# Sliding-window attention and a gated FFN on one core: separate PSUM tensors for single banks, key copies on ScalarE

## The chip, the core and the metric

The kernel runs on one core of a Trainium2 chip. Engines of a core run their own instruction queues in order and meet at semaphores: TensorE (PE: matmuls; PEld: its weight loads), VectorE (DVE), ScalarE (ACT), GpSimd (POOL) and SyncE (SP), which here issues the transfers from and to device memory. PE writes its results to PSUM, eight banks of 2 KB per partition; DVE and ACT read them from there. The metric is the device time of one execution in microseconds; the measured time before is the median of three runs.

## The reference

```
scores = scale * q @ k^T ; keep = (pos_k < 4) | (0 <= pos_q - pos_k < 128)
a = softmax(where(keep, scores, -1e9)) ; x = a @ v        # 4 batches, 8 heads, 768 positions, head size 64
y = (relu(X @ w_gate) * (X @ w_val)) @ w_out              # X: 3072 x 512, d_ff 1536
```

Each position attends to the first four keys ("sink") and to the 128 keys up to itself. The heads are then put side by side and go through the FFN.

## The kernel before

Two heads make a pair; there are 16 pairs (`U[0]` to `U[15]`), four to a batch. For a pair, `T` transposes keys and queries on PE (8 + 8 transposes, keys first) into PSUM and copies them to SBUF: the keys into `kE` by five copies (L178 and L181 on DVE, L180 twice on ACT, and L183 on DVE, which copies the four sink columns from `kE` itself to three further places), the queries into `qT` by one copy on DVE (L182). `Sg(u, g)`, three for a pair, makes the scores of a window group (L196) in both banks of a two-bank tensor, and ACT takes their exponentials (L200); DVE multiplies them by a mask (L202), except in the head, where a bias matmul (L192) masks them. `V(u, part)`, two for a pair, multiplies by the values into one bank and by ones into the other, for the row sums (L213); DVE then transposes the sums, inverts them, transposes back and multiplies (L219 to L223) into `xT`.

`chunk(b, g, m)` is the first FFN layer for 384 positions and 128 of the 1536 columns: four gate matmuls (L235) into bank `gp`, the relu on ACT into `gs` (L238), four value matmuls (L240) into bank `vp`, and the product of `gs` and `vp` on DVE into `hT` (L242). The banks `gp` and `vp` go round three: bank 0 and 1 of `ps0` and bank 0 of `ps1` (`GV`). `ffn2` is one of twelve matmuls of the second layer (L255) into bank 1 of `ps1` (`OP`); after the twelfth, ACT copies the result (L259) and SP stores it.

All eight banks are four tensors `ps0` to `ps3` of two banks. In the head, `T`, `Sg` and `V` go round all four (`nextps`); afterwards round `ps2` and `ps3`.

The order is written out by hand. The head does pairs 0 to 3, then loads and casts the FFN weights. Then come 96 slots, one per chunk: batch 0 in slots 0 to 23, batch 1 from slot 24 on, and so on. After its chunk a slot runs steps of the attention of the next batch in the order T, S, S, S, V, V for each pair: from slot 12 to 23 two steps a slot (pairs 4 to 7), from slot 24 to 71 one step a slot (pairs 8 to 15), after that none. From slot 24 on a slot ends with three `ffn2` matmuls. The 72 that are left over run at the end without a chunk. The waits on the semaphores are put in by the framework, from the tensors that an instruction reads and writes.

Of the kernel before, what the change touches and what calls it, by code (L numbers as in the profile page):

```python
# [9 lines left out]
F32 = mybir.dt.float32  # L10
# [9 lines left out]
def kernel(  # L20
# [48 lines left out]
    mb = const.tile([128, 3, 512], BF16, name="mb")  # L69
    PS = [pspool.tile([128, 2, 512], F32, name=f"ps{i}") for i in range(4)]  # L70
    GV = [PS[0][:, 0, :], PS[0][:, 1, :], PS[1][:, 0, :]]

# [86 lines left out]

    rot = [0]  # L160
    banks = [PS]

    def nextps():
        rot[0] += 1
        return banks[0][rot[0] % len(banks[0])]

    def T(u):
        t = u.i % NT
        ps = nextps()[:].bitcast(BF16)
        for j, x in ((1, kn[u.i % 2]), (0, qn[u.i % 2])):  # L170
            for n in range(NR):
                nc.tensor.transpose(ps[:, j, 96 * n:96 * n + 96],  # L172
                                    x[0:PR, n, :, :].rearrange("p h d -> p (h d)"), ident[0:PR, 0:PR])
        vk, vq = (ps[:, j, 0:768].rearrange("d (b p) -> d p b", p=PR) for j in (1, 0))
        n_ = dict(b=8)
        to = lambda ap: ap.rearrange("d (p b) -> d p b", **n_)
        e = kE[t]
        nc.vector.tensor_copy(to(e[:, 0:128]), vk[:, 0:16])  # L178
        for i in range(2):
            nc.scalar.copy(to(e[:, 132 + 252 * i:380 + 252 * i]), vk[:, 16 + 31 * i:47 + 31 * i])  # L180
        nc.vector.tensor_copy(to(e[:, 636:780]), vk[:, 78:96])  # L181
        nc.vector.tensor_copy(to(qT[t][:]), vq)  # L182
        nc.vector.tensor_copy(e[:, 128:884].rearrange("d (i c) -> d i c", c=252)[:, :, 0:4],  # L183
                              e[:, 0:4].unsqueeze(1).to_broadcast([128, 3, 4]))

    def Sg(u, g, bias=False):
        t = u.i % NT
        n, segs = SEG[g]
        ps = nextps()
        if bias:  # L190
# [71 lines left out]
    with tc.manual_schedule():  # L262
# [132 lines left out]
```

## Time and profile before

| | before |
|---|---|
| median of 3 runs (lowest to highest) | 359.69 us (357.64 to 360.26) |
| profiled execution: time, span | 357.96 us, 356.3 us |
| PE busy | 276.0 us (77%) |
| DVE busy | 173.6 us (49%) |
| ACT busy | 116.0 us (33%) |
| POOL busy | 71.9 us (20%) |
| mean granted PE clock | 0.951 |
| chain that ended last: PE, DVE, ACT | 59%, 16%, 8% |

The span is the time between the first and the last instruction of the profile. A group of matmuls is drawn to its modelled end, so that the next group can start before the drawn end of the one ahead of it. "Idle <- X" at a row names what ended the idle time in front of it.

### The profile page before, as it was taken

Reading aid. Unit: us, or ns where it says so; the run is one execution under the profiler, and the core shown is the slowest. Engines: PE = TensorE matmul, PEld = TensorE weight load, DVE = VectorE, ACT = ScalarE, POOL = GpSimd, SP = SyncE. Lnnn points to the kernel's source line nnn. Section 1 sums busy time; section 2 is a strip of 40 time slices with the busy share of each in tenths; the row PEclk is TensorE's granted clock in tenths of the full one; section 3 lists DMA queues with packets and bytes.
Section 4 is the critical chain, followed back from the end, with each engine's and each line's share of the span. In section 5 each row is a group of like instructions: output and inputs, shape, how many; then the busy total and the mean of one; then the engine's idle time right before and its main releaser. Section 6 shows DMA issues by size and latency. Waiting matters only on the chain.

```text
span 356.3 us, 5404 instructions
## 1 busy us (share of the span) xinstructions
PE 276.0 (77%) x2114; PEld 148.3 (42%) x2136; DVE 173.6 (49%) x348; ACT 116.0 (33%) x202; POOL 71.9 (20%) x90
## 2 busy tenths in 40 slices
PE   1868287655965888898888889897989788878895
PEld 1336143324533444454444535353545344434442
DVE  4677623268557665656464737465646122221100
ACT  2535022232442443434334352425152222222211
POOL 5366500893033030303030302100000000000000
PEclk9989679969888799999999999999999999999999
DMA  8999999399560005107230520000000000000032
GB/s 200 237 272 351 286 210 309 137 234 193 113 136 0 2 1 154 33 10 163 92 74 31 138 56 3 31 29 0 31 31 29 0 31 29 29 29 31 2 118 88
DMA packets 44105, 35.14 MB, mean 99 GB/s; under 512 B 27184, under 2 KB 33328, under 8 KB 44080
## 3 DMA queue, kind: packets, MB, share of 16 engines
q1 hardware_dynamic: 44080, 34.81, 38.6%
q8 instruction: 16, 0.26, 0.3%
q14 instruction: 9, 0.07, 0.1%
HBM read 28.51 MB, written 6.29 MB: 98 GB/s over the span
## 4 chain that ended last, share of the span: by engine, by line
PE 59%; DVE 16%; ACT 8%; issue 5%; DMA 5%; SPq 2%; POOL 2%; ACTq 0%; DVEq 0%; POOLq 0%
PE ps L255 17%; PE ps L240 15%; PE ps L235 14%; PE ps L213 5%; PE ps L196 4%; DVE hT L242 4%; ACT gs L238 4%; DVE qT L182 3%; PE ps L172 3%; DMA wst<-in_moe_w_out_dram 3%; DMA vf<-in_v_dram 2%; ACT kE L180 2%; ACT ot L259 2%; DVE R L221 2%; DVE t L219 2%
## 5 line engine op out<-in xcount | busy, mean ns | idle before, releaser
L242 DVE TENSOR_TENSOR hT<-gs,ps 128x384 bf16<-128x384 f32 x96 | 53.1, 553 | 104.9 <-PE ps L240 104.4
L240 PE MATMUL ps<-xT,wv 128*128 128x384 bf16 x384 | 81.9, 337 | 21.5 <-ACT gs L238 20.7
L235 PE MATMUL ps<-xT,wg 128*128 128x384 bf16 x384 | 82.6, 339 | 14.4 <-DVE xT L223 6.8
L238 ACT ACTIVATE gs<-ps 128x384 f32<-128x384 f32 x96 | 47.1, 491 | 127.3 <-PE ps L235 126.4
L255 PE MATMUL ps<-wo,hT 128*128 128x512 bf16 x266 | 71.4, 380 | 10.1 <-DVE hT L242 8.9
L240 PEld LDWEIGHTS <-wv 128*128 128x128 bf16 x384 | 38.5, 100 | 56.8 <-issue 35.9
L200 ACT ACTIVATE ee<-ps 128x1006 bf16<-128x1006 f32 (+2 forms) x48 | 45.1, 961 | 40.7 <-PE ps L196 40.7
L235 PEld LDWEIGHTS <-wg 128*128 128x128 bf16 x384 | 37.4, 100 | 50.3 <-issue 21.8
L111 POOL CAST kn<-kf 96x1024 bf16<-96x1024 f32 x16 | 16.6, 1035 | 115.8 <-PE ps L172 112.7
L255 PEld LDWEIGHTS <-hT 128*128 128x128 bf16 x288 | 25.0, 97 | 35.3 <-issue 13.9
L202 DVE TENSOR_TENSOR ee<-ee,msk 128x1006 bf16<-128x1006 bf16 (+2 forms) x36 | 25.2, 700 | 28.6 <-ACT ee L200 28.4
L196 PE MATMUL ps<-qT,kE 64*128 64x251 bf16 (+4 forms) x224 | 21.7, 281 | 16.5 <-DVE qT L182 13.8
L196 PEld LDWEIGHTS <-kE 64*128 64x128 bf16 x224 | 10.5, 101 | 35.4 <-issue 30.0
L180 ACT COPY kE<-ps 128x248 bf16<-128x248 bf16 x32 | 10.1, 369 | 41.2 <-DVE kE L178 41.1
L259 ACT COPY ot<-ps 128x512 f32<-128x512 f32 x24 | 14.0, 583 | 27.3 <-PE ps L255 24.2
L219 DVE STREAM_TRANSPOSE t<-ps 128x384 f32<-128x384 f32 x32 | 18.6, 580 | 5.9 <-PE ps L213 4.8
L221 DVE STREAM_TRANSPOSE R<-r 128x384 f32<-128x384 f32 x32 | 18.5, 578 | 1.1
L223 DVE TENSOR_TENSOR xT<-ps,R 128x384 bf16<-128x384 f32 x32 | 17.8, 557 | 1.1
L213 PE MATMUL ps<-ee,vn 128*64 128x255 bf16 (+8 forms) x288 | 16.1, 236 | 0.9 <-DVE xT L223 0.9
L104 POOL CAST vn<-vf 128x896 bf16<-128x896 f32 x16 | 14.8, 926 | 8.2 <-DMA vf<-in_v_dram 8.2
L213 PEld LDWEIGHTS <-vn 128*64 128x64 bf16 x288 | 12.5, 110 | 7.6 <-issue 7.2
L213 PE MATMUL ps<-ee,ones 128*64 128x255 bf16 (+8 forms) x288 | 15.6, 233 | 0.0
(43 smaller groups left out, 144.1 us busy)
## 6 DMA issues: line engine op xcount, KB each, us to landing
kf<-in_k_dram SPq DMA_DIRECT2D x16, 384.0 KB
qf<-in_q_dram SPq DMA_DIRECT2D x16, 384.0 KB
vf<-in_v_dram SPq DMA_DIRECT2D x32, 192.0 KB
out_dram<-ot SPq DMA_DIRECT2D x24, 256.0 KB
wst<-in_moe_w_gate_dram SPq DMA_DIRECT2D x6, 512.0 KB
wst<-in_moe_w_val_dram SPq DMA_DIRECT2D x6, 512.0 KB
wst<-in_moe_w_out_dram SPq DMA_DIRECT2D x3, 1024.0 KB
vf<-in_v_dram SPq DMA_DIRECT2D x16, 12.0 KB
```

What stands on the lines that cost most here:

```text
L196: nc.tensor.matmul(out=ps[:, h, c0:c1], lhsT=kE[t][64 * h:64 * h + 64, x0:x0 + 128], rhs=qT[t][64 * h:64 * h + 64, q0:q0 + c1 - c0], start ...
L200: nc.scalar.activation(x, ps[:, :, 0:n], Act.Exp, bias=0.0, scale=scale)
L202: nc.vector.tensor_tensor(x, x, msk[:, g, 0:n].unsqueeze(1).to_broadcast([128, 2, n]), op=Alu.mult)
L213: nc.tensor.matmul(out=ps[64 * h:64 * h + 64, which, o0:o0 + c1 - c0], lhsT=w, rhs=ee[u.i % NE][:, g, h, c0:c1], start=i == 0, stop=i == l ...
L219: nc.vector.transpose(out=t1[:], in_=ps[:, 1, 0:CUT])
L221: nc.vector.transpose(out=R[:].rearrange("p (c e) -> p c e", e=32), in_=r[:].unsqueeze(2).to_broadcast([128, CUT // 32, 32]))
L235: nc.tensor.matmul(out=gp[:, 0:CUT], lhsT=wg[:, ko, m * 128:(m + 1) * 128], rhs=x[:, ko, c], start=ko == 0, stop=ko == KO - 1)
L238: nc.scalar.activation(gs[:], gp[:, 0:CUT], Act.Relu, bias=0.0, scale=1.0)
L240: nc.tensor.matmul(out=vp[:, 0:CUT], lhsT=wv[:, ko, m * 128:(m + 1) * 128], rhs=x[:, ko, c], start=ko == 0, stop=ko == KO - 1)
L242: nc.vector.tensor_tensor(h[:, m, c], gs[:], vp[:, 0:CUT], op=Alu.mult)
L255: nc.tensor.matmul(out=op, lhsT=hT[b % 2][:, m, t * 128:(t + 1) * 128], rhs=wo[:, m, :], start=m == 0, stop=m == FM - 1)
L259: nc.scalar.copy(ot[:], op)
```

## The change

The eight banks are cut differently: two tensors of two banks, `PP` (`pp0`, `pp1`), and four of one bank, `G` (`g0` to `g3`). The first layer of the FFN goes round `g0`, `g1`, `g2`, the second layer writes `g3`: the same number of banks for each as before, each now with a tensor of its own. The scores take a whole `PP` tensor. `T` transposes the keys into one tensor and the queries into another, and `V` puts values and sums, in the head, into two `G` tensors; after the head, `V` takes both banks of one `PP` tensor, and `T` one bank of each. In the head, `T` and `V` go round the `G` tensors and the scores round the two `PP` tensors. All key copies of a pair, that of the sink columns too, go to ACT; the query copy stays on DVE and comes first.

```diff
-    PS = [pspool.tile([128, 2, 512], F32, name=f"ps{i}") for i in range(4)]
-    GV = [PS[0][:, 0, :], PS[0][:, 1, :], PS[1][:, 0, :]]
+    PP = [pspool.tile([128, 2, 512], F32, name=f"pp{i}") for i in range(2)]
+    G = [pspool.tile([128, 512], F32, name=f"g{i}") for i in range(4)]
...
-    def nextps():
-        rot[0] += 1
-        return banks[0][rot[0] % len(banks[0])]
+    def pair():
+        rot[0] += 1
+        return PP[rot[0] % 2]
+
+    def two():
+        if head[0]:
+            srot[0] += 2
+            return G[srot[0] % 4][:], G[(srot[0] + 1) % 4][:]
+        x = pair()
+        return x[:, 0, :], x[:, 1, :]
...
     def T(u):
-        ps = nextps()[:].bitcast(BF16)
-        for j, x in ((1, kn[u.i % 2]), (0, qn[u.i % 2])):
+        tk, tq = two() if head[0] else (pair()[:, 0, :], pair()[:, 0, :])
+        for x, ps in ((kn[u.i % 2], tk), (qn[u.i % 2], tq)):
...
-        nc.vector.tensor_copy(to(e[:, 0:128]), vk[:, 0:16])
+        nc.vector.tensor_copy(to(qT[t][:]), vq)
+        nc.scalar.copy(to(e[:, 0:128]), vk[:, 0:16])
         for i in range(2):
             nc.scalar.copy(to(e[:, 132 + 252 * i:380 + 252 * i]), vk[:, 16 + 31 * i:47 + 31 * i])
-        nc.vector.tensor_copy(to(e[:, 636:780]), vk[:, 78:96])
-        nc.vector.tensor_copy(to(qT[t][:]), vq)
-        nc.vector.tensor_copy(e[:, 128:884].rearrange("d (i c) -> d i c", c=252)[:, :, 0:4],
-                              e[:, 0:4].unsqueeze(1).to_broadcast([128, 3, 4]))
+        nc.scalar.copy(to(e[:, 636:780]), vk[:, 78:96])
+        nc.scalar.copy(e[:, 128:884].rearrange("d (i c) -> d i c", c=252)[:, :, 0:4],
+                       e[:, 0:4].unsqueeze(1).to_broadcast([128, 3, 4]))
...
-        gp, vp = GV[gvn[0] % 3], GV[(gvn[0] + 1) % 3]
+        gp, vp = G[gvn[0] % 3], G[(gvn[0] + 1) % 3]
...
-    OP = [[PS[1][:, 1, :]], [PS[1][:, 1, :], PS[2][:, 0, :], PS[3][:, 0, :]]]
+    OP = [[G[3][:]], [G[3][:], PP[0][:, 0, :], PP[1][:, 0, :]]]
```

`Sg` takes `pair()` where it took `nextps()`, and `V` takes `two()`. Because lines are added, L172 becomes L180, L196 L203, L200 L207, L213 L220, L235 L242, L238 L245, L240 L247, L242 L249, L255 L262 and L259 L266.

No engine's instructions change in number or place but for those of `T` on DVE and ACT. What changes elsewhere are the waits. The first place is PE in the last FFN batch (slots 80 and 81), the first matmul of each group and what it waits for. Before (`wg`: gate, `wv`: value, `wo`: second layer; the number of a semaphore's name means nothing):

```order
L235 MATMUL ps0_110<-xT1_102,wg_98 128x384 [waits DVE_49]
...
L240 MATMUL ps1_111<-xT1_102,wv_99 128x384 [waits Activation_49]
...
L255 MATMUL ps1_111<-wo_100,hT0_103 128x512 [waits DVE_49]
...
L235 MATMUL ps0_110<-xT1_102,wg_98 128x384 [waits Activation_49]
...
L240 MATMUL ps0_110<-xT1_102,wv_99 128x384 [waits Activation_49]
```

After:

```order
L242 MATMUL g1_113<-xT1_102,wg_98 128x384 [waits DVE_49]
...
L247 MATMUL g2_114<-xT1_102,wv_99 128x384 [waits Activation_49]
...
L262 MATMUL g3_115<-wo_100,hT0_103 128x512 [waits Activation_49]
...
L242 MATMUL g0_112<-xT1_102,wg_98 128x384 [waits DVE_49]
...
L247 MATMUL g1_113<-xT1_102,wv_99 128x384 [waits Activation_49]
```

The same rows in the same order, but the second-layer matmul no longer waits for DVE, and the value matmuls of the last row write a tensor (`g1`) that the gate matmuls ahead of them (`g0`) do not write and their relu does not read.

The second place is `T` of pair 5 on DVE, between the product of one chunk and the next one's. Before:

```order
L242 TENSOR_TENSOR hT0_103<-gs_881,ps0_110 128x384 [waits PE_49,Activation_49]
L178 COPY kE2_87<-ps3_113 128x128 [waits PE_49]
L181 COPY kE2_87<-ps3_113 128x144 [waits Activation_49]
L182 COPY qT2_84<-ps3_113 128x768
L183 COPY kE2_87<-kE2_87 128x3x4 [waits DVE_49]
L202 TENSOR_TENSOR ee2_90<-ee2_90,msk_108 128x2x503 [waits Activation_49]
```

After:

```order
L249 TENSOR_TENSOR hT0_103<-gs_883,g1_113 128x384 [waits PE_49,Activation_49]
L185 COPY qT2_84<-pp1_111 128x768 [waits PE_49]
L209 TENSOR_TENSOR ee2_90<-ee2_90,msk_108 128x2x503 [waits Activation_49]
L249 TENSOR_TENSOR hT0_103<-gs_931,g0_112 128x384 [waits PE_49,Activation_49]
L209 TENSOR_TENSOR ee2_90<-ee2_90,msk_108 128x2x499 [waits Activation_49]
```

Three copies left DVE's queue, and the query copy follows the product of the chunk at once. On ACT, at the same place, before:

```order
L238 ACTIVATE gs_881<-ps0_110 128x384 [waits PE_49,Activation_49]
L180 COPY kE2_87<-ps3_113 128x248 [waits DVE_49]
L180 COPY kE2_87<-ps3_113 128x248
L200 ACTIVATE ee2_90<-ps2_112 128x2x503 [waits PE_49]
L238 ACTIVATE gs_929<-ps1_111 128x384 [waits PE_49,Activation_49]
```

After (the row that ends in x2 stands for the two copies of 248 columns):

```order
L245 ACTIVATE gs_883<-g0_112 128x384 [waits PE_49]
L186 COPY kE2_87<-pp0_110 128x128 [waits DVE_49,PE_49]
L188 COPY kE2_87<-pp0_110 128x248 x2
L189 COPY kE2_87<-pp0_110 128x144
L190 COPY kE2_87<-kE2_87 128x3x4 [waits Activation_49]
L207 ACTIVATE ee2_90<-pp0_110 128x2x503 [waits PE_49]
```

The copies now stand on ACT in one run, and wait for PE and an earlier instruction of DVE, not for a copy of the same pair on DVE.

The third place is PE at `T` of pair 5 and the scores behind it. Before (first key transpose, first query transpose, then the loads and the matmul of the scores):

```order
L172 MATMUL ps3_113<-ident_105,kn1_94 128x96 [waits DVE_49]
...
L172 LDWEIGHTS qn1_92 [waits Pool_49]
...
L196 LDWEIGHTS kE2_87 [waits DVE_49]
L196 MATMUL ps2_112<-qT2_84,kE2_87 128x255 [waits DVE_49]
...
L196 LDWEIGHTS kE2_87 [waits DVE_49,Activation_49]
```

After:

```order
L180 MATMUL pp0_110<-ident_105,kn1_94 128x96 [waits DVE_49]
...
L180 MATMUL pp1_111<-ident_105,qn1_92 128x96 [waits DVE_49]
...
L203 LDWEIGHTS kE2_87 [waits DVE_49,Activation_49]
L203 MATMUL pp0_110<-qT2_84,kE2_87 128x255 [waits Activation_49]
...
L203 LDWEIGHTS kE2_87 [waits Activation_49]
```

The query transposes go to the other tensor and got a wait on DVE of their own; the scores now wait for ACT's copies too where they waited for DVE's.

## Rows read from the trace of the kernel before

**Rows 1.** By stretch: us; PE, PEld, DVE, ACT, POOL busy; clock; DMA; GB/s
```profile
41.70:70.50 28.80, 21.85 (x104) 10.69 (x103) 7.20 (x13) 6.38 (x13) 8.48 (x10) 0.88 0.95 224
70.50:125.50 55.00, 37.61 (x361) 22.19 (x361) 37.26 (x71) 18.98 (x32) 19.55 (x24) 0.81 0.53 110
125.50:276.00 150.50, 128.88 (x1045) 71.18 (x1060) 88.01 (x170) 57.47 (x100) 20.34 (x24) 1.00 0.20 54
276.00:336.30 60.30, 48.49 (x247) 24.13 (x249) 12.79 (x24) 14.21 (x28) 0.00 (x0) 1.00 0.06 22
```
**Rows 2.** What PE waited for from 125.5 to 337 us: total, times, longest
```profile
PE ps L240 <- ACT gs L238: 14.7, 23, 0.6
PE ps L255 <- DVE hT L242: 8.9, 16, 0.7
PE ps L235 <- ACT ot L259: 4.1, 6, 0.7
PE ps L196 <- DVE qT L182: 2.4, 8, 0.3
PE ps L196 <- DVE kE L183: 1.5, 6, 0.3
```
**Rows 3.** PE's timeline, last FFN batch: start, length, instructions, [idle <-releaser]
```profile
285.89 0.81 PE L255 MATMUL ps<-wo,hT 128*128 128x512 bf16 x3
...
287.26 0.81 PE L240 MATMUL ps<-xT,wv 128*128 128x384 bf16 x4
288.79 0.81 PE L255 MATMUL ps<-wo,hT 128*128 128x512 bf16 x3 [0.72 <-DVE hT L242]
289.44 0.81 PE L235 MATMUL ps<-xT,wg 128*128 128x384 bf16 x4
290.89 0.81 PE L240 MATMUL ps<-xT,wv 128*128 128x384 bf16 x4 [0.64 <-ACT gs L238]
...
293.63 0.81 PE L255 MATMUL ps<-wo,hT 128*128 128x512 bf16 x3
```
**Rows 4.** Timeline, a middle pair: last V step, transposes, next chunk, first scores
```profile
181.03 0.56 DVE L223 TENSOR_TENSOR xT<-ps,R 128x384 bf16<-128x384 f32 x1
...
182.52 0.50 PE L172 MATMUL ps<-ident,qn 96*128 96x96 bf16 x8
...
184.16 0.81 PE L240 MATMUL ps<-xT,wv 128*128 128x384 bf16 x4
...
185.28 0.28 PE L196 MATMUL ps<-qT,kE 64*128 64x255 bf16 x2 [0.31 <-DVE qT L182]
```
**Rows 5.** Timeline of pair 6, first FFN batch: from V to scores
```profile
98.96 0.56 DVE L223 TENSOR_TENSOR xT<-ps,R 128x384 bf16<-128x384 f32 x1
99.44 0.54 DVE L242 TENSOR_TENSOR hT<-gs,ps 128x384 bf16<-128x384 f32 x1
...
99.90 0.28 DVE L178 COPY kE<-ps 128x128 bf16<-128x128 bf16 x1
100.22 0.63 ACT L180 COPY kE<-ps 128x248 bf16<-128x248 bf16 x2 [2.94 <-DVE kE L178]
...
101.11 0.95 DVE L182 COPY qT<-ps 128x768 bf16<-128x768 bf16 x1
...
102.11 0.45 PE L196 MATMUL ps<-qT,kE 64*128 64x255 bf16 x4 [3.29 <-DVE qT L182]
```
**Rows 6.** Timeline around pair 4: POOL casts, transposes, sink copy
```profile
62.22 2.02 POOL L129 CAST wo<-wst 128x1024 bf16<-128x1024 f32 x2 [17.40 <-DMA wst<-in_moe_w_out_dram]
...
69.47 1.04 POOL L111 CAST kn<-kf 96x1024 bf16<-96x1024 f32 x1
...
70.56 0.51 PE L172 MATMUL ps<-ident,kn 96*128 96x96 bf16 x8 [0.80 <-POOL kn L111]
...
74.17 1.63 DVE L183 COPY kE<-kE 128x12 bf16<-128x12 bf16 x1
```
**Rows 7.** Timeline, the second-layer matmuls at the end
```profile
336.30 16.35 PE L255 MATMUL ps<-wo,hT 128*128 128x512 bf16 x74 [0.72 <-DVE hT L242]
```

More of the change, by code (lines that the diff above doesn't have):

```diff
@@ L158, in setup @@
             nc.vector.tensor_scalar(mb[:, g, 0:n], msk[:, g, 0:n], -1.0, BIG, op0=Alu.add, op1=Alu.mult)
-    rot = [0]
-    banks = [PS]
-    def nextps():
+    rot, srot = [0], [0]
+    head = [True]
+    def pair():
         rot[0] += 1
-        return banks[0][rot[0] % len(banks[0])]
+        return PP[rot[0] % 2]
[5 more added lines that the diff above has]
+        return x[:, 0, :], x[:, 1, :]
     def T(u):
         t = u.i % NT
-        ps = nextps()[:].bitcast(BF16)
-        for j, x in ((1, kn[u.i % 2]), (0, qn[u.i % 2])):
+        tk, tq = two() if head[0] else (pair()[:, 0, :], pair()[:, 0, :])
+        for x, ps in ((kn[u.i % 2], tk), (qn[u.i % 2], tq)):
             for n in range(NR):
-                nc.tensor.transpose(ps[:, j, 96 * n:96 * n + 96],
+                nc.tensor.transpose(ps.bitcast(BF16)[:, 96 * n:96 * n + 96],
                                     x[0:PR, n, :, :].rearrange("p h d -> p (h d)"), ident[0:PR, 0:PR])
-        vk, vq = (ps[:, j, 0:768].rearrange("d (b p) -> d p b", p=PR) for j in (1, 0))
-        n_ = dict(b=8)
-        to = lambda ap: ap.rearrange("d (p b) -> d p b", **n_)
+        vk, vq = (ps.bitcast(BF16)[:, 0:768].rearrange("d (b p) -> d p b", p=PR) for ps in (tk, tq))
         e = kE[t]
-        nc.vector.tensor_copy(to(e[:, 0:128]), vk[:, 0:16])
+        to = lambda ap: ap.rearrange("d (p b) -> d p b", b=NR)
+        nc.vector.tensor_copy(to(qT[t][:]), vq)
+        nc.scalar.copy(to(e[:, 0:128]), vk[:, 0:16])
         for i in range(2):
             nc.scalar.copy(to(e[:, 132 + 252 * i:380 + 252 * i]), vk[:, 16 + 31 * i:47 + 31 * i])
-        nc.vector.tensor_copy(to(e[:, 636:780]), vk[:, 78:96])
-        nc.vector.tensor_copy(to(qT[t][:]), vq)
-        nc.vector.tensor_copy(e[:, 128:884].rearrange("d (i c) -> d i c", c=252)[:, :, 0:4],
-                              e[:, 0:4].unsqueeze(1).to_broadcast([128, 3, 4]))
+        nc.scalar.copy(to(e[:, 636:780]), vk[:, 78:96])
+        nc.scalar.copy(e[:, 128:884].rearrange("d (i c) -> d i c", c=252)[:, :, 0:4],
+                       e[:, 0:4].unsqueeze(1).to_broadcast([128, 3, 4]))
     def Sg(u, g, bias=False):
@@ L188, in Sg @@
         n, segs = SEG[g]
-        ps = nextps()
+        ps = pair()
         if bias:
@@ L206, in V @@
     def V(u, part):
-        ps = nextps()
+        pv, pd = two()
         segs = VSEG[part]
@@ L212, in V @@
                     w = vn[u.i % NV][:, j, h, :] if which == 0 else ones[:]
-                    nc.tensor.matmul(out=ps[64 * h:64 * h + 64, which, o0:o0 + c1 - c0], lhsT=w,
+                    nc.tensor.matmul(out=(pv, pd)[which][64 * h:64 * h + 64, o0:o0 + c1 - c0], lhsT=w,
                                      rhs=ee[u.i % NE][:, g, h, c0:c1], start=i == 0, stop=i == len(segs) - 1,
@@ L218, in V @@
         r = npool.tile([128, CUT // 32], F32, name="r")
-        nc.vector.transpose(out=t1[:], in_=ps[:, 1, 0:CUT])
+        nc.vector.transpose(out=t1[:], in_=pd[:, 0:CUT])
         nc.vector.reciprocal(r[:], t1[:].rearrange("p (c e) -> p c e", e=32)[:, :, 0])
@@ L222, in V @@
                             in_=r[:].unsqueeze(2).to_broadcast([128, CUT // 32, 32]))
-        nc.vector.tensor_tensor(xT[u.b % 2][:, u.p, CUT * part:CUT * part + CUT], ps[:, 0, 0:CUT], R[:], op=Alu.mult)
+        nc.vector.tensor_tensor(xT[u.b % 2][:, u.p, CUT * part:CUT * part + CUT], pv[:, 0:CUT], R[:], op=Alu.mult)
         ready[u.b, u.p, part] = True
@@ L305 @@
             cast_wo(c, c, nc.gpsimd)
-        banks[0] = PS[2:4]
+        head[0] = False
         stages = []
```

## Prediction

> **What bounds the kernel now.** I read the busy time by stretch first, then PE's waits, then the timelines behind the largest waits.
>
> By stretch [rows 1]: from 125.5 us on, PE is 80 to 86% busy at full clock, and DVE (58% and 21%), ACT (38% and 24%) and the transfers (20% and less) are far from full. So PE is the bound there, with holes. From 70.5 to 125.5 PE is 68% busy at a mean clock of 0.81, and DVE 68%: two in-order queues that wait for each other. From 41.7 to 70.5 the transfers are at 95%.
>
> The holes after 125.5 us have names [rows 2]. The largest is the value matmuls (L240) waiting for the relu (L238), 14.7 us in 23 waits. The value matmuls do not use the relu's result; the gate and value banks of that chunk are the two banks of `ps0`. Nor do the second-layer matmuls use the product that they wait for (L255 <- L242, 8.9 us in 16): the one writes a bank of `ps1`, the other reads the other bank. The same holds for the gate matmuls waiting for the output copy (4.1 in 6). These are waits for a neighbour bank of the same tensor.
>
> What a slot costs without them is in [rows 3]: the gate matmuls at 289.44 start 0.65 us after the three second-layer matmuls at 288.79, though these are drawn 0.81 long. So a hole is 0.16 us longer than its row says. The four value matmuls behind gates with no wait take 0.65 too. Three slots take 293.63 - 285.89 = 7.74 us; dense they would take 3 x 3 x 0.65 = 5.9.
>
> **The change part by part.**
>
> *One tensor per bank in the FFN.* The listing of the last batch shows what is left: gate matmuls wait for the DVE product of two chunks earlier (their bank's last reader), value matmuls for the relu of the chunk before, the first second-layer matmul of a block for the output copy. With slots of about 2 us, each of these was done a slot ago or, for the output copy, within the next chunk's 1.3 us (the gates right behind it wait 4.1 / 6 = 0.7 us for it now). I cost them at nothing. Removed: the five lines of [rows 2] are 31.6 us in 59 waits, and 59 x 0.16 = 9.4 us behind them, 41 in all. The other way round, PE is idle for 150.50 + 60.30 - 128.88 - 48.49 = 33.4 us of the two stretches [rows 1], and with the same 9.4 that makes 42.8. Of these the last batch has 8 x (7.74 - 5.9) = 14.7 (24 slots), which leaves 28 for the 8 pairs of the middle: a pair there goes from 150.5 / 8 = 18.8 to 15.3 us. I take 43.
>
> *The copies of T, after 125.5 us.* The last two lines of [rows 2] (2.4 and 1.5, counted above) are the scores waiting for query and sink copy. ACT's run of five copies is not in the trace as a whole. The two of 248 columns take 0.63 [rows 5]. Each of the three new ones (128 and 144 columns, and 12) costs at least 0 and at most half of that, 0.32: the run is 0.63 to 1.6. I take 1.3, nearest to the upper end, since a small copy has a fixed part. Its cover is what PE does between the last key transpose and the scores: from 182.52 to 184.16 + 0.65 = 184.81, 2.29 us [rows 4]. Hidden; the relu of the next chunk waits behind the run, but its reader on PE comes a chunk later. DVE loses three copies per pair that were on nobody's path here.
>
> *A new wait.* The query transposes now go to the tensor that the last V step leaves, and wait for its last DVE instruction. Behind them on PE stand the second layer and the next chunk. In [rows 4] that instruction ends at 181.03 + 0.56 = 181.59; the transposes start at 182.52, of which 0.64 us is a relu wait (a line like the last L240 of [rows 3]) that goes: 181.88. Slack 0.29. Cost 0, at most 0.3 x 8 = 2.4.
>
> *Pairs 4 to 7, 70.5 to 125.5 us.* Here the scores follow `T` at once, so the copies are on the path. Before [rows 5]: the product ends at 99.98, then key copy, ACT's two copies, key copy, query copy one after the other, and the scores start at 102.11. After: the query transposes may start when V's last step ends, 99.52, take 0.34 (drawn 0.50 in [rows 4], less the 0.16) and about 0.2 until DVE has them, the copy takes 0.95: 101.0. That is 1.1 us for each of pairs 5, 6 and 7, 3.3 in all; ACT's run, at most 1.6 from 0.34 earlier on, ends at about the same time. For pair 4 the sink copy, which took 1.63 us on DVE beside POOL's casts [rows 6], also goes to ACT: 1.63, less some 0.4 that the first scores cover, and the 1.1 as for the others, about 2.3. The last chunk of the stretch loses a relu wait: 0.8. Together 6.4. Bounds: 3, if only pair 4 and a part of the rest come through, and 10, if PE, less interrupted, is at full clock for one more chunk per pair (a chunk is 1.3 us at full clock and twice that at the lower level; mean clock 0.81 [rows 1]).
>
> *The head and 41.7 to 70.5 us: nothing.* The 13 chunks there lose their relu waits too. But the next thing on PE is `T` of pair 4, and that waits for POOL's key cast at 69.47, behind the casts of the output weights, the first of which waited 17.40 us for its transfer [rows 6]. The transfers are at 95% [rows 1] and the change moves none of them. PE will stand still before 70.5 instead: 28.8 us of the stretch less 13 x 1.3 us, and less what the lower clock takes, some 8 us. For the same reason the head's scores, which now have two tensors instead of four, cost nothing: a head later by up to those 8 us would not show.
>
> Sum: 357.96 (the profiled execution's own time, 1.7 us under the median of the runs shown and inside their spread) - 43 - 6.4 = 308.6. I say 308 us.
>
> **A rule against it.** In [rows 5] a key copy of 128 columns takes 0.28 us on DVE, and two of 248 columns take 0.63 on ACT: 2.2 and 1.3 ns per column, so ACT is not the slower engine for this. The Trainium skill, "ScalarE: Activation LUTs", section Rules for kernel authors, says the opposite for plain arithmetic: use VectorE, which is up to about three times faster per element in bf16. By that the three moved copies would make the run late, which is the second rival below. The rows speak for the forecast.
>
> **The rivals.**
> 1. *The waits come back elsewhere.* With slots of 1.96 us instead of 2.58, ACT and DVE answer as late as before, and some product or relu ends up last in each slot. For it: chains of ACT and DVE are as long as before, and where a slot has scores, ACT has relu, exponential and at times an output copy, near 2 us. Against: each wait left has a whole slot of slack. If half of the 43 us returns, 308 + 21 = 329.
> 2. *ACT's run of key copies is late.* Were each moved copy three times DVE's 0.28 us, the run would be 0.63 + 2.5 = 3.1: 0.8 over its cover of 2.29 for 8 pairs, and about 1.6 over the query path of 1.5 (0.34 + 0.2 + 0.95) for 4 pairs: 6.4 + 6.4, 321 us. Against: the nanoseconds per column of [rows 5].
> 3. *The change does not do what it says*: the waits stay, since they came from something other than the tensor. Then only the copies count: 357.96 - 6 = 352, or nothing. Against: the second-layer row in the listing has lost its wait for DVE, and the value row its tensor.
> 4. *Slower: the denser PE is granted less clock.* From about 118 us to the end, some 180 us of PE work would run nearly without holes, which this kernel never did before for so long. At the lower of the two levels they would take twice as long. It ends slower than before once 49/180 = 27% of that work runs at the lower level; all of it, 308 + 180 = 488. Against: the 74 second-layer matmuls at the end run back to back, 16.35 us, 0.22 each [rows 7], which is the full level, and from 125.5 to 336.3 the clock is 1.00 [rows 1].
>
> **How the numbers follow.** The forecast has 72 in 100 and spans 300 to 315: 41 to 44 for the holes, 3 to 10 for pairs 4 to 7, up to 2.4 for the new wait. The second rival has 8, up to 321. The first has 10 (321 to 340), the third 3, the fourth 4; 3 are left for below 300, if the pairs 4 to 7 gain more than I see. So 300 to 321 holds 80. A measurement of this kernel can tell about 1% from no change. Faster by over 1%: 72 + 8 + 10 + 3 and 1 of the third, 94; within 1%: 2 of the third; slower: the fourth, 4.
>
> **What would show it.** Value matmuls with no idle time behind a relu, slots of 1.95 to 2.0 us in the last batch, a pair each 15.3 us in the middle, and at most a few us of PE waits after 125 us. `T` of pair 4 at 70 to 71 us as before, with 7 to 9 us of idle PE ahead of it. Pairs 5 to 7 each 1 to 2 us shorter than before. ACT's run of copies 1.0 to 1.6 us. Query transposes with no wait, or one of some 0.1 us, in the middle. I would be wrong if the second layer or the values still waited in each slot (first rival), if `T` of pair 4 moved, or if the clock after 125 us fell below 1.00.

## The result, and the profile after

The changed kernel takes 309.29 us (median of 4 runs, 307.69 to 311.3), the kernel before, measured beside it, 359.34 us: a ratio of 0.8615, interval 0.8546 to 0.8683. The forecast was 308 us, with 300 to 315 as its range (72 in 100) and 300 to 321 with the second rival (80 in 100). Some runs hold an execution or two over 1.5% slower than the fastest of the same kernel; the ratios leave these out, the medians in us do not. The execution whose profile is read below took 308.14 us, with a span of 306.4.

| | before | after |
|---|---|---|
| span of the profiled execution | 356.3 us | 306.4 us |
| PE busy | 276.0 us (77%) | 264.9 us (86%) |
| DVE busy | 173.6 us (49%) | 160.2 us (52%) |
| ACT busy | 116.0 us (33%) | 123.6 us (40%) |
| chain that ended last: PE, DVE, ACT | 59%, 16%, 8% | 71%, 10%, 2% |

In the changed file the query copy is L185, the key copies are L186 to L190, and the last DVE instruction of `V` is L230.

By stretch, in the columns of [rows 1], after the change:

```profile
42.30:68.60 26.30, 18.74 (x104) 10.66 (x103) 7.20 (x14) 6.38 (x13) 8.14 (x9) 0.84 0.94 234
68.60:117.20 48.60, 37.76 (x357) 21.62 (x358) 32.09 (x56) 20.42 (x43) 20.00 (x23) 0.81 0.55 124
117.20:241.00 123.80, 121.86 (x1042) 68.90 (x1057) 81.76 (x147) 60.97 (x124) 20.38 (x24) 1.00 0.24 63
241.00:287.00 46.00, 45.74 (x256) 25.36 (x260) 13.86 (x26) 14.77 (x30) 0.00 (x0) 1.00 0.09 35
```

From 117 us on PE is 98 to 99% busy, and all that it still waited for between 119 and 287 us is in two lines, which answer to the five of [rows 2] (total, times, longest; "issue" is time for which the profile shows no cause):

```profile
PE pp L180 <- DVE xT L230: 0.6, 1, 0.6
PE g L262 <- issue: 0.6, 4, 0.2
```

The last FFN batch, to be laid beside [rows 3]:

```profile
245.46 0.81 PE L262 MATMUL g<-wo,hT 128*128 128x512 bf16 x3
246.11 0.81 PE L242 MATMUL g<-xT,wg 128*128 128x384 bf16 x4
246.76 0.81 PE L247 MATMUL g<-xT,wv 128*128 128x384 bf16 x4
247.41 0.81 PE L262 MATMUL g<-wo,hT 128*128 128x512 bf16 x3
...
251.30 0.81 PE L262 MATMUL g<-wo,hT 128*128 128x512 bf16 x3
```

Three slots take 251.30 - 245.46 = 5.84 us instead of 7.74, with nothing in brackets.

**Where the time went.** Two instants cut each profile into three: the start of `T` of pair 4, and the first scores of pair 8, by which the second FFN batch has begun. The second instant in the timeline of before (start, length, instructions, [idle <-releaser]):

```profile
128.60 0.28 PE L196 MATMUL ps<-qT,kE 64*128 64x255 bf16 x2 [0.31 <-DVE qT L182]
```

and after:

```profile
121.36 0.39 PE L203 MATMUL pp<-qT,kE 64*128 64x255 bf16 x4
```

| us | T of pair 4 starts | from there to the scores of pair 8 | from there to the end |
|---|---|---|---|
| before | 70.56 | 58.04 | 227.7 |
| after | 68.61 | 52.75 | 185.0 |
| gone | 1.95 | 5.3 | 42.7 |

The three sum to 49.9, the difference of the spans.

### The profile page after: what moved, and what is told of

Read it like the earlier page. It is cut to its first block, busy times and chain, and to the rows that moved or that the text cites. A ratio compares the mean times of both kernels' runs of the same rounds, so it can differ in the third digit from the quotient of the medians.

```text
span 306.4 us, 5389 instructions
## 1 busy us (share of the span) xinstructions
PE 264.9 (86%) x2114; PEld 147.6 (48%) x2136; DVE 160.2 (52%) x300; ACT 123.6 (40%) x250; POOL 72.7 (24%) x90
## 4 chain that ended last, share of the span: by engine, by line
PE 71%; DVE 10%; DMA 8%; SPq 3%; ACT 2%; issue 2%; POOL 2%; DVEq 0%; ACTq 0%; POOLq 0%
PE g L262 18%; PE g L242 17%; PE g L247 17%; PE pp L203 5%; PE pp L220 4%; PE pp L262 3%; DMA wst<-in_moe_w_out_dram 3%; DMA vf<-in_v_dram 3%; PE pp L180 2%; PE pp L199 2%; DMA qf<-in_q_dram 2%; ACT ee L207 2%; DVE R L228 2%; DVE xT L230 2%; DVE t L226 2%
## 5 line engine op out<-in xcount | busy, mean ns | idle before, releaser
L249 DVE TENSOR_TENSOR hT<-gs,g 128x384 bf16<-128x384 f32 x96 | 53.1, 553 | 68.2 <-PE g L247 67.3
L245 ACT ACTIVATE gs<-g 128x384 f32<-128x384 f32 x96 | 47.2, 491 | 98.4 <-PE g L242 88.3
L242 PE MATMUL g<-xT,wg 128*128 128x384 bf16 x384 | 82.2, 338 | 4.1 <-DVE xT L230 4.1
L247 PE MATMUL g<-xT,wv 128*128 128x384 bf16 x384 | 81.6, 337 | 0.0
L262 PE MATMUL g<-wo,hT 128*128 128x512 bf16 x218 | 61.0, 381 | 1.6 <-issue 0.6
L207 ACT ACTIVATE ee<-pp 128x1006 bf16<-128x1006 f32 (+2 forms) x48 | 45.4, 959 | 32.6 <-PE pp L203 32.5
L242 PEld LDWEIGHTS <-wg 128*128 128x128 bf16 x384 | 37.4, 100 | 37.4 <-issue 6.9
L247 PEld LDWEIGHTS <-wv 128*128 128x128 bf16 x384 | 38.8, 101 | 28.6 <-issue 5.2
L262 PEld LDWEIGHTS <-hT 128*128 128x128 bf16 x288 | 24.5, 98 | 24.8 <-issue 3.3
L203 PE MATMUL pp<-qT,kE 64*128 64x251 bf16 (+4 forms) x224 | 20.1, 282 | 4.6 <-DVE qT L185 4.6
L203 PEld LDWEIGHTS <-kE 64*128 64x128 bf16 x224 | 8.1, 100 | 22.5 <-issue 17.2
L266 ACT COPY ot<-g 128x512 f32<-128x512 f32 x20 | 11.7, 583 | 15.8 <-PE g L262 15.8
L220 PEld LDWEIGHTS <-vn 128*64 128x64 bf16 x288 | 12.8, 110 | 10.0 <-issue 8.9
L180 PEld LDWEIGHTS <-kn 96*128 96x128 bf16 x128 | 7.9, 107 | 18.9 <-POOL kn L112 14.8
L185 DVE COPY qT<-pp 128x768 bf16<-128x768 bf16 x12 | 11.5, 957 | 9.6 <-PE pp L180 8.7
L226 DVE STREAM_TRANSPOSE t<-pp 128x384 f32<-128x384 f32 x24 | 13.9, 579 | 2.5 <-PE pp L220 1.7
L230 DVE TENSOR_TENSOR xT<-pp,R 128x384 bf16<-128x384 f32 x24 | 13.4, 557 | 0.8
L180 PE MATMUL pp<-ident,kn 96*128 96x96 bf16 x96 | 6.4, 211 | 8.1 <-POOL kn L112 7.5
```

The source lines that it names most:

```text
L180: nc.tensor.transpose(ps.bitcast(BF16)[:, 96 * n:96 * n + 96], x[0:PR, n, :, :].rearrange("p h d -> p (h d)"), ident[0:PR, 0:PR])
L203: nc.tensor.matmul(out=ps[:, h, c0:c1], lhsT=kE[t][64 * h:64 * h + 64, x0:x0 + 128], rhs=qT[t][64 * h:64 * h + 64, q0:q0 + c1 - c0], start ...
L207: nc.scalar.activation(x, ps[:, :, 0:n], Act.Exp, bias=0.0, scale=scale)
L220: nc.tensor.matmul(out=(pv, pd)[which][64 * h:64 * h + 64, o0:o0 + c1 - c0], lhsT=w, rhs=ee[u.i % NE][:, g, h, c0:c1], start=i == 0, stop= ...
L226: nc.vector.transpose(out=t1[:], in_=pd[:, 0:CUT])
L242: nc.tensor.matmul(out=gp[:, 0:CUT], lhsT=wg[:, ko, m * 128:(m + 1) * 128], rhs=x[:, ko, c], start=ko == 0, stop=ko == KO - 1)
```

## The experiments

The first four take the change apart; a table behind them collects their pieces.

**1. The FFN banks alone.** The changed kernel with the old `T`:

```diff
-        tk, tq = two() if head[0] else (pair()[:, 0, :], pair()[:, 0, :])
+        tk, tq = two()
...
-        nc.vector.tensor_copy(to(qT[t][:]), vq)
-        nc.scalar.copy(to(e[:, 0:128]), vk[:, 0:16])
+        nc.vector.tensor_copy(to(e[:, 0:128]), vk[:, 0:16])
...
-        nc.scalar.copy(to(e[:, 636:780]), vk[:, 78:96])
+        nc.vector.tensor_copy(to(e[:, 636:780]), vk[:, 78:96])
+        nc.vector.tensor_copy(to(qT[t][:]), vq)
```
(the sink copy goes back to `nc.vector` too)

> The changed kernel with only the step T put back: after the head its keys and queries are transposed into the two banks of one tensor again, and the copies are VectorE, ScalarE, ScalarE, VectorE, VectorE (queries), VectorE (sink) as before. The FFN banks stay tensors of their own. Theory: the 42 us of holes after 119 us stay gone, and only what pairs 4 to 7 gained by the copies (about 4 of the 5.7 us there; the last chunk's 0.8 and the uninterrupted value matmuls stay) is lost: 313 to 315 us, with scores behind the value step 6.6 us again in pairs 5 to 7 and no wait of the query transposes for VectorE. Rival (the copies don't matter, pairs 4 to 7 gained by the FFN alone): 309. Also read: when T of pair 4 starts, 68.6 us as after or 70.6 as before; if 70.6, its 1.95 us come from the copies' place or chance, if 68.6, from the FFN part or chance.

Measured: 320.77 us, ratio to before 0.8904 (0.8839 to 0.8969). The old `T` costs 11.5 us against the 309.29 of the changed kernel (10.4 by the ratios), where 4 to 6 were expected: a miss. Two places show it, in the profile of an execution of 323.51 us, 2.7 above the median. After the scores of pair 8 there are waits again that the expectation had left out, though [rows 2] has them in its last two lines:

```profile
PE pp L203 <- DVE qT L189: 3.0, 8, 0.9
PE pp L203 <- DVE kE L190: 1.3, 5, 0.3
```

Ahead of them, in pair 6, the scores come 6.60 us behind the first DVE instruction of the value steps in front of them (97.93 to 104.53), as expected. DVE's timeline there, in the columns of [rows 5]:

```profile
101.86 0.54 DVE L249 TENSOR_TENSOR hT<-gs,g 128x384 bf16<-128x384 f32 x1
102.32 0.28 DVE L185 COPY kE<-pp 128x128 bf16<-128x128 bf16 x1
103.31 0.31 DVE L188 COPY kE<-pp 128x144 bf16<-128x144 bf16 x1 [0.70 <-ACT kE L187]
103.53 0.95 DVE L189 COPY qT<-pp 128x768 bf16<-128x768 bf16 x1
```

and PE's behind it:

```profile
104.53 0.61 PE L203 MATMUL pp<-qT,kE 64*128 64x255 bf16 x4 [3.65 <-DVE qT L189]
105.07 1.46 PE L242 MATMUL g<-xT,wg 128*128 128x384 bf16 x4
```

DVE stands 0.70 us in the middle of `T`, since its second key copy writes behind ACT's two, and the query copy is last; both were so before. PE, which no longer stops for the relu, is at this point earlier and stands 3.65 us (2.74 to 3.29 before, in pairs 5 to 7); behind that pause four gate matmuls take 1.46 us, as before in pairs 5 and 7 (0.94 in pair 6). From one pair's scores to the next it takes 13.66 to 13.68 us at a granted clock of 0.75 to 0.79, where the changed kernel takes 12.90, 12.11 and 11.36 at 0.76, 0.87 and 1.00. So the loss goes beyond the 0.9 us by which the path is longer, and comes with the lower clock; that it comes from it is not shown by this run. Part of this profile's excess over the median may be pair 4's start at 71.97, 3.4 us behind that of the changed kernel.

**2. The copies alone.** The kernel before, its four two-bank tensors kept:

```diff
+        nc.vector.tensor_copy(to(qT[t][:]), vq)
-        nc.vector.tensor_copy(to(e[:, 0:128]), vk[:, 0:16])
+        nc.scalar.copy(to(e[:, 0:128]), vk[:, 0:16])
...
-        nc.vector.tensor_copy(to(e[:, 636:780]), vk[:, 78:96])
-        nc.vector.tensor_copy(to(qT[t][:]), vq)
+        nc.scalar.copy(to(e[:, 636:780]), vk[:, 78:96])
```
(and the sink copy to `nc.scalar`)

> The kernel before with only the order and the engine of T's copies changed (query copy first on VectorE, all five key copies on ScalarE); the four two-bank tensors stay. Theory: the holes after 119 us stay, with some 31 us in the same five lines of PE waits; pair 4 loses the sink copy's 1.63 us on VectorE, pairs 5 to 7 a few tenths each, since both copies still wait for the last transpose: 354 to 357 us. Rival (the change's gain is largely from the copies): under 345. Rival (ScalarE's run of five is late and costs): over 360.

Measured: 353.39 us, ratio 0.9846 (0.9779 to 0.9913), 5.5 us of gain against the 358.91 of the kernel before beside it, and 0.6 us below the expected range. The three large lines of [rows 2] stay (14.8, 9.2 and 4.1 us); the two small ones, for query and sink copy, are gone.

**3. The tensors put back.** The changed kernel, same banks, same instructions in the same order:

```diff
-    G = [pspool.tile([128, 512], F32, name=f"g{i}") for i in range(4)]
+    GG = [pspool.tile([128, 2, 512], F32, name=f"gg{i}") for i in range(2)]
+    G = [GG[i // 2][:, i % 2, :] for i in range(4)]
```

> The changed kernel with only the declaration of its four FFN banks put back: two tensors of two banks each, the same banks in the same places, the same instructions in the same order. Theory (PE waits for a neighbour bank of one tensor): the holes come back, value matmuls wait for the relu again in each chunk, second layer for the product: 309 + 42 = 351, at least 345. Rival (the waits went because of the new order of banks or the copies, not the tensors): 309.

Measured: 347.27 us, ratio 0.9652 (0.959 to 0.9714): 38 us more than the changed kernel by this declaration alone. PE's waits from 123 to 326 us:

```profile
PE gg L248 <- ACT gs L246: 14.2, 23, 0.6
PE gg L263 <- DVE hT L250: 8.9, 16, 0.7
PE gg L243 <- ACT ot L267: 4.1, 6, 0.7
PE gg L248 <- ACT ot L267: 0.5, 3, 0.2
PE gg L263 <- ACT gs L246: 0.3, 1, 0.3
```

The first three are those of [rows 2] again, to 0.5 us each. All five are 28.0 us in 49 waits; with the forecast's 0.16 behind each, 35.8. The rival, that the order of banks or the copies had taken them away, falls.

**4. One shared pair.** Banks 0 and 1 in one tensor, 2 and 3 alone:

```diff
-    G = [pspool.tile([128, 512], F32, name=f"g{i}") for i in range(4)]
+    G01 = pspool.tile([128, 2, 512], F32, name="g01")
+    G2, G3 = (pspool.tile([128, 512], F32, name=f"g{i}") for i in (2, 3))
+    G = [G01[:, 0, :], G01[:, 1, :], G2[:], G3[:]]
```

> The changed kernel with banks 0 and 1 of the FFN in one two-bank tensor, banks 2 and 3 tensors of their own: a dose between the changed kernel and the run with two shared pairs. Of three chunks in a row one has gate and value in the shared tensor, one has its gate in bank 2 and its value in bank 0, one its gate in bank 1 and its value in bank 2. Theory: only the first kind waits for its relu, 0.64 + 0.16 = 0.8 us in each third chunk; the 71 chunks from 119 us on have 24 of these: 19 us, 325 to 330 in all; gate matmuls of the third kind may wait for the product of the chunk before (bank 0), up to as much again. Rival (waits are by bank): 309.

Measured: 330.06 us, ratio 0.9183 (0.9121 to 0.9246). From 125 to 311 us one line is left:

```profile
PE g L249 <- ACT gs L247: 14.2, 23, 0.6
```

Only the chunks whose gate and value share the tensor wait, and only for the relu. The second layer, now in a bank of its own, waits for nothing, and the gates do not wait for the product of the chunk before.

The first four together, with the changed kernel:

| us | time | T of pair 4 | to the scores of pair 8 | to the end |
|---|---|---|---|---|
| before | 359.34 | 70.56 | 58.04 | 227.7 |
| copies alone (2) | 353.39 | 70.85 | 55.53 | 224.3 |
| all of `T`, FFN in two-bank tensors (3) | 347.27 | 70.74 | 52.58 | 222.0 |
| all of `T`, one shared pair (4) | 330.06 | 71.59 | 53.64 | 204.7 |
| FFN banks alone, old `T` (1) | 320.77 | 71.97 | 59.89 | 189.9 |
| changed | 309.29 | 68.61 | 52.75 | 185.0 |

By the times, the FFN tensors are worth 38 us with the new `T` (347.27 - 309.29) and 38 without it (358.91, the kernel before as measured beside these runs, - 320.77). The new `T` is worth 11.6 us without the FFN tensors (358.91 - 347.27) and 11.5 with them. By the ratios it is 37 and 39 us, 12.5 and 10.4. So the two parts add up, 38 + 11.6 = 49.6, to within some 2 us. Of the 11.6, 5.5 come from the engines and order of the copies, 6.1 from what else differs between runs 2 and 3: the different tensors for keys and queries, and which banks the head uses. That it is the tensors of keys and queries is argued; no run has them alone. By the pieces: the FFN tensors give 37.0 us behind the scores of pair 8 and nothing ahead of them (52.58 and 52.75); with the old `T` the stretch is 1.85 longer with them (58.04 to 59.89), but two profiles of the changed kernel differ by 0.83 there (run 9) and that of run 1 is of an execution above its median, so how much of the 1.85 is theirs is not shown. The new `T` gives 5.5 ahead and 5.7 behind, with the FFN tensors 7.1 and 4.9.

**5. The output weights later.** In the changed kernel, for the part of the first step that was costed at nothing:

```diff
-            cast_wo(c, c, nc.gpsimd)
...
+            if s in (14, 16, 18):
+                cast_wo((s - 14) // 2, (s - 14) // 2, nc.gpsimd)
```

> The changed kernel with the casts of the output weights moved from ahead of the FFN to behind its chunks 14, 16 and 18, so that on POOL the casts of pair 4's keys and queries no longer stand behind them. Transfers and everything else stay. Theory (pair 4's keys are held by POOL's queue alone, PE stands 7.5 us for them): T of pair 4 starts right behind the 13 chunks at about 61 us instead of 68.6, and what follows moves with it: 309.3 - 7.5 = 302 us, T at 61 to 62 and no idle ahead of it. Rival (the transfers hold something else that is late next, the values or keys of pairs 5 to 7, or the casts now fall beside DVE's work and slow it): 305 to 309 with the idle time moved behind. This run also says what of T's earlier start in the changed kernel, 68.6 for 70.6, hangs on when the output weights land: here nothing should.

Measured: 300.18 us as the median of four, of which the ratio counts the two of 297 us: 0.8276 (0.8211 to 0.8341), 5 us better than expected and some 12 less than the changed kernel.

```profile
58.66 0.81 PE L247 MATMUL g<-xT,wv 128*128 128x384 bf16 x4
59.31 0.51 PE L180 MATMUL pp<-ident,kn 96*128 96x96 bf16 x8
```

`T` of pair 4 starts at 59.31 us right behind the chunks, 9.3 earlier than in the changed kernel; from there to the scores of pair 8 it is 50.99 us, 1.8 less, and 185.1 to the end. What shortens that stretch no run here takes alone. Pair 4's keys were held by their place in POOL's queue, behind casts that waited 16 to 18 us for a transfer, and by nothing else.

**6. Attention spread.** Besides, one step of attention behind each chunk from the first on:

```diff
-                want.append(max(0, s - 11) * 2)
+                want.append(s + 1)
```

> As the run with the output weights later, and the steps of attention of pairs 4 to 7 stand one behind each chunk from the first of batch 0, instead of two behind each from chunk 12. Theory: pairs 4 to 7 are a chain DVE -> T -> scores -> DVE with too little beside it on PE; with a chunk of 1.3 us between any two steps PE has cover for the 5.7 us from the value step to the next scores, and batch 1 begins when 24 chunks (31 us) and four pairs of attention (3.5 us each) are done, some 90 to 95 us instead of 117: 281 to 288 us. Rival (keys and values of pairs 5 to 7 come late by their transfers, or DVE is the bound with some 8 us a pair): batch 1 begins at 105 or later, 295 to 303.

Measured: 289.64 us, ratio 0.8097 (0.8027 to 0.8168), and 290.2 (0.8091, 0.8054 to 0.8128) when run again beside run 8:

> The spread kernel once more, beside the one with the queries in the free bank: 289 to 290 us, and four waits of the query transposes for VectorE of about 0.6 us.

The times lie between theory and rival. Batch 1 begins behind the last value step of pair 7, which starts at 96.44 us: 2 to 7 us later than expected, of which 2.7 and 1.0 are `T` of pair 4 waiting for its keys and queries, since it now comes so early that it is their transfers that hold it. The later pairs stand 12.2 to 12.3 us apart, and PE works at full clock from 53 us on. Each query transpose waits for DVE, as the row of pair 5 shows; in the second run these waits were 0.59 to 1.18:

```profile
62.90 0.50 PE L180 MATMUL pp<-ident,qn 96*128 96x96 bf16 x8 [0.59 <-DVE xT L230]
```

**7. The pauses filled.** Matmuls whose result nobody reads, in the changed kernel:

```diff
+            if 4 < u.i < 8:
+                for _ in range(fill):
+                    nc.tensor.matmul(out=G[3][:], lhsT=ident[:], rhs=wg[:, 0, 0:512], start=True, stop=True)
```
(behind the eight transposes of the keys `fill` is 6, behind those of the queries 4)

> The changed kernel with matmuls that serve nothing in the pauses of PE in pairs 5, 6 and 7: six of 128x512 into the free bank 3 behind the key transposes, four behind the query transposes; nothing reads them. They are 1.3 and 0.9 us at full clock for pauses of 1.5 and 1.1 us. Theory (these pairs gained less than forecast since PE, standing longer, comes back at the lower clock: groups of four chunk matmuls draw 1.46 us instead of 0.82): with the pauses filled the groups behind the scores are at 0.82, each of three pairs is 1 to 2 us shorter, and batch 1 begins 3 to 6 us earlier: 303 to 306 us. Rival (the lower level comes from something else, or DVE's chain alone sets the pairs): 309 to 312, the groups behind the scores still at 1.46.

Measured: 306.77 us, ratio 0.8559 (0.8507 to 0.8611), against 0.8615 and, in run 9, 0.8651 for the changed kernel. The interval overlaps that of the first and meets that of the second, so the times alone do not settle it; the traces do. The changed kernel, pair 5:

```profile
83.35 0.50 PE L180 MATMUL pp<-ident,qn 96*128 96x96 bf16 x8 [1.46 <-DVE xT L230]
84.99 0.61 PE L203 MATMUL pp<-qT,kE 64*128 64x255 bf16 x4 [1.14 <-DVE qT L185]
85.53 1.46 PE L242 MATMUL g<-xT,wg 128*128 128x384 bf16 x4
86.78 1.48 PE L247 MATMUL g<-xT,wv 128*128 128x384 bf16 x4
88.20 0.95 PE L203 MATMUL pp<-qT,kE 64*128 64x251 bf16 x10
```

and with the fill:

```profile
84.07 1.46 PE L184 MATMUL g<-wg,ident 128*128 128x512 bf16 x6
85.69 0.50 PE L180 MATMUL pp<-ident,qn 96*128 96x96 bf16 x8 [0.16 <-DVE xT L233]
86.03 1.03 PE L184 MATMUL g<-wg,ident 128*128 128x512 bf16 x4
87.33 0.39 PE L206 MATMUL pp<-qT,kE 64*128 64x255 bf16 x4 [0.28 <-DVE qT L188]
87.66 0.82 PE L245 MATMUL g<-xT,wg 128*128 128x384 bf16 x4
88.32 0.81 PE L250 MATMUL g<-xT,wv 128*128 128x384 bf16 x4
89.06 0.57 PE L206 MATMUL pp<-qT,kE 64*128 64x251 bf16 x10
```

The scores come no sooner behind the transposes (1.64 us in both), but what follows them runs at the higher of the two levels instead of the lower. From one pair's scores to the next it takes 10.63 and 10.62 us (pairs 5 to 6 and 6 to 7), where the changed kernel takes 12.90 and 12.11. From the scores of pair 7 to those of pair 8 it is 11.36 us in both: behind the same two pauses the changed kernel stays at the higher level there (groups of 0.82), and the fill gains nothing. So here it acts where the clock had fallen, and only there. From `T` of pair 4 to the scores of pair 8 it is 48.98 us, 3.8 less, though 30 matmuls more are done. The time shows less of it, 2.5 us; in the profile `T` of pair 4 started at 70.96, 2.35 us later than in the changed kernel's own.

**8. The queries into a free bank.** In the kernel of run 6:

```diff
-        tk, tq = two() if head[0] else (pair()[:, 0, :], pair()[:, 0, :])
+        tk, tq = two() if head[0] else (pair()[:, 0, :], G[3][:] if u.i < 2 * NP else pair()[:, 0, :])
```

> The spread kernel (one step of attention behind each chunk) with one more change: in pairs 4 to 7 the queries are transposed into bank 3, which is free in batch 0, instead of the tensor that the value step before leaves. So nothing of T waits for VectorE's last value instruction. Theory: the wait that the change brought with the new tensor (0.59 to 0.66 us in each of pairs 5 to 7 of the spread kernel, with 0.16 behind it) goes from these three: 3 x 0.8 = 2.3 us, some 287 us against 289.6; the fourth, in pair 8, stays. Rival (the wait hides others: the scores would then wait for the query copy or the values for VectorE): 289 to 290, with as much idle time a few instructions later.

Measured: 287.68 us, ratio 0.7991 (0.7948 to 0.8034), against 290.2 for run 6 beside it. The waits of the query transposes of pairs 5 to 7 are gone, but the scores wait instead:

```profile
65.52 0.39 PE L203 MATMUL pp<-qT,kE 64*128 64x255 bf16 x4 [1.61 <-DVE qT L185]
77.78 0.39 PE L203 MATMUL pp<-qT,kE 64*128 64x255 bf16 x4 [0.71 <-DVE qT L185]
89.99 0.39 PE L203 MATMUL pp<-qT,kE 64*128 64x255 bf16 x4 [0.66 <-DVE qT L185]
```

The rival held in the trace: DVE works in order and takes the query copy behind its value step all the same, so the pairs still stand 12.2 us apart (89.99 - 77.78). `T` of pair 4 began 2.2 us earlier than in the second run of 6 (45.76 and 47.95), ahead of anything the edit touches, but by the scores of pair 5 that is used up (65.52 and 65.62). From `T` of pair 8 on both take 188.4 us, and the spans differ by 0.7 (287.8 and 288.5): 0.6 of it is the one long wait of run 6 (1.18 us, pair 6), twice the others. The profile is of an execution of 289.54 us, 1.9 above the median. The intervals of the two ratios do not touch, but these traces show no place for 2.5 us: whether they come from the edit stays open.

**9. The changed kernel again**, unaltered, for the 1.95 us by which `T` of pair 4 had moved:

> The changed kernel once more, unaltered. Its profile had pair 4's T start at 68.61 us, 1.95 earlier than before the change, when the forecast was no shift. Theory (that is the scatter of when the output weights land, not the change): another profile of the same kernel has it anywhere in 68 to 72 us, and the landing moves with it; time 307 to 312. Rival (the change brings it forward): 68.4 to 68.8 again.

Measured: 310.38 us, ratio 0.8651 (0.8611 to 0.8691). Up to that instant run 7 is the same program too, so there are three readings. The changed kernel's first profile:

```profile
68.61 0.82 PE L180 MATMUL pp<-ident,kn 96*128 96x96 bf16 x8 [7.51 <-POOL kn L112]
```

its second, of this run:

```profile
69.27 0.82 PE L180 MATMUL pp<-ident,kn 96*128 96x96 bf16 x8 [7.98 <-POOL kn L112]
```

and run 7:

```profile
70.96 0.82 PE L180 MATMUL pp<-ident,kn 96*128 96x96 bf16 x8 [9.97 <-POOL kn L112]
```

One program starts it anywhere over 2.35 us, as the first cast of the output weights moves (60.25, 60.94 and 62.50 us). Before it was 70.56: inside that band. So the 1.95 us are no more than the scatter of one program, and cannot be put down to the change. From `T` of pair 4 to the scores of pair 8 this profile has 53.58 us, where the first has 52.75, and from there to the end 185.0 in both.

## Why the prediction was right

**The holes after 125.5 us: 43 forecast, 42.7 measured.** Both ways of counting them, by the listed waits and by PE's idle time, gave the size, because what took their place was nothing: 0.6 us in one wait and 0.6 of issue. Runs 3 and 4 settle the mechanism: the instructions and banks of the changed kernel, with only the tensors joined, bring the waits back, and one joined pair of two brings back 23 waits. The price of a wait, its row and 0.16 us behind it, held too: run 4 has 204.7 - 185.0 = 19.7 us for 23 waits, 0.86 each, where 0.64 + 0.16 = 0.8 was the price. Slots of 1.95 us, a pair of 15.3 (here from 134.00 to 149.37, 15.37) and the clock of 1.00 came as forecast. The list had a sixth line, of 0.7 us in 4 waits, which [rows 2] leaves out; it changes the count by 1.3. Of the 43, some 6 were the scores' waits for query and sink copy, which the forecast counted here, though they belong to the new `T`; runs 3 and 1 put them there (5.7 and 4.9 us).

**Pairs 4 to 7: 6.4 forecast, 5.3 measured (4.5 in the profile of run 9), and by another sum.** The path that was drawn is there: the query transposes start when the last V step ends, the copy follows. From V's first DVE instruction to the scores it is 5.70 us (104.30 to 110.00) and was 6.60: 0.9 for the 1.1 of the forecast. But the pairs did not each become 1 to 2 us shorter. From one pair's scores to the next, with the mean granted clock:

| us (clock) | before | changed | changed, run 9 | with the fill, run 7 |
|---|---|---|---|---|
| pair 4 to 5 | 14.75 (0.84) | 13.43 (0.75) | 13.57 (0.75) | 13.42 (0.88) |
| pair 5 to 6 | 13.05 (0.87) | 12.90 (0.76) | 12.59 (0.77) | 10.63 (1.00) |
| pair 6 to 7 | 12.71 (0.81) | 12.11 (0.87) | 11.98 (0.88) | 10.62 (1.00) |
| pair 7 to 8 | 13.78 (0.81) | 11.36 (1.00) | 12.49 (0.86) | 11.36 (1.00) |

What was missed is how far the clock moves from pair to pair. Behind pair 5 it is lower than before, and 0.15 us is left of the gain; behind pair 7 it did not fall in the first profile, and 2.42 us are gained, nearly half of the 5.3, where 0.8 was forecast for the relu wait. The bound of 10 named that gain ("PE, less interrupted, is at full clock for one more chunk per pair"); it came in one pair, and in another the reverse. Run 7 sizes it: the lower clock costs the changed kernel 2.3 and 1.5 us in pairs 5 and 6, and nothing from pair 4 to 5, where 13.42 us stand beside 13.43. For pair 4's sink copy 2.3 were forecast; the scores there came 2.95 us behind the first transpose, and 3.75 before, with 1.24 more at the second scores, but only 1.32 of a gain shows from there to pair 5. That the total came near is luck in part.

**ACT's run of key copies: 1.3 forecast, 1.07 measured**, from 118.37 to the end of the last row:

```profile
118.37 0.27 ACT L186 COPY kE<-pp 128x128 bf16<-128x128 bf16 x1 [0.50 <-PE pp L180]
118.53 0.64 ACT L188 COPY kE<-pp 128x248 bf16<-128x248 bf16 x2
119.04 0.31 ACT L189 COPY kE<-pp 128x144 bf16<-128x144 bf16 x1
119.21 0.23 ACT L190 COPY kE<-kE 128x12 bf16<-128x12 bf16 x1
```

So the second rival, a late run, did not come. The moved copies cost the same on either engine: 0.27 us here and 0.28 on DVE for 128 columns, 0.31 and 0.31 for 144 (run 1). The Trainium skill, "ScalarE: Activation LUTs", Rules for kernel authors, would have plain arithmetic on VectorE, up to about three times faster per element in bf16 (for single-source operations in a mode it calls 4x). For these copies out of PSUM the trace shows nothing of that factor: 0.27 us beside 0.28.

**The new wait: nothing in the middle, as forecast** (one wait of 0.6 us, at pair 8). Where PE runs dense with attention spread over batch 0, in run 6, it does show, 0.6 us a pair; run 8 shows that it stands for DVE's order there, not for the tensor.

**`T` of pair 4: fixed at 70.56 in the forecast, 68.61 in the profile.** The idle time ahead of it came as forecast (7.51 of "some 8" us), and run 5 shows the cause that was given: `T` starts 9.3 us earlier once POOL takes that pair's keys first, and the span is 11.0 shorter (306.4 to 295.4). Only the instant is not as fixed as the forecast took it: run 9 has its scatter.

**The other rivals.** The waits did not come back elsewhere. The change did what it says. The clock did not fall under a dense PE (1.00 from 117 us to 287); in the rows above it is low behind a stop of PE.

The two fastest kernels of these runs are: attention spread with the output weights later, 290 us, and the same with the queries in the free bank, 287.7 (ratio 0.7991).

## What to carry to other kernels

When an engine waits for a result that it does not use, look whether the two sides share a tensor: here neighbours in one two-bank tensor cost 38 of 347 us (run 3), and a declaration took that away. Read a gain stage by stage: where two engines wait for each other, taking waits from the one that is not late gave nothing here (52.58 and 52.75 us), and the in-order queue of the other (POOL's casts, DVE's copies) is what to reorder. A change that moves the slow transfers' readers in a queue can be worth as much as one on the engine that is the bound (some 12 us in run 5 and another 6 in run 6, by the ratios).

## What the runs showed that was not expected

Useless work made a stretch faster. In pairs 5 and 6 of the changed kernel two pauses of 1.46 and 1.14 us, with eight transposes between, are followed by groups of four matmuls of 1.46 us; with ten matmuls of 128x512 that serve nothing in them the same groups take 0.82, and a pair is 1.5 to 2.3 us shorter (10.63 and 10.62 for 12.90 and 12.11). The Trainium skill, "TensorE: Matmul & The Clock Gate", section "A second HAM failure mode: psum-queue depth-cycling", tells of a kernel whose short idle times between groups of matmuls make the clock go down and up again and again; the granted clock of 0.76 and 0.87 in these two pairs agrees. But the same pauses do not always do it. Behind those of pair 7 the groups of the first profile stay at the higher level:

```profile
110.00 0.39 PE L203 MATMUL pp<-qT,kE 64*128 64x255 bf16 x4 [1.14 <-DVE qT L185]
110.32 0.82 PE L242 MATMUL g<-xT,wg 128*128 128x384 bf16 x4
110.98 0.81 PE L247 MATMUL g<-xT,wv 128*128 128x384 bf16 x4
```

and in that of run 9 the fall comes one group later:

```profile
110.68 0.82 PE L242 MATMUL g<-xT,wg 128*128 128x384 bf16 x4
111.34 1.30 PE L247 MATMUL g<-xT,wv 128*128 128x384 bf16 x4
```

What decides it no run here shows.

The landing of the output weights scatters: over the eight profiles of kernels that cast them ahead of the FFN (before and the changed kernel, the latter twice, and runs 1 to 4 and 7), `T` of pair 4 started between 68.61 and 71.97 us. A shift of 2 us at this place of one profile says nothing until a second profile of the same program has it.
